# A bias column in a channel product, and PSUM copies of the first head pairs on one engine

## The chip, the cores and the metric

The kernel runs on one core of a Trainium2 chip. The metric is the device time of one execution in microseconds (us), as the median of several runs. A profile is one execution recorded by the hardware; its own time is given beside its span (first to last instruction). Engines are named as in the profile: PE is TensorE (matrix products; PEld are its weight loads), ACT is ScalarE, DVE is VectorE, POOL is GpSimd, SP is SyncE, which here only issues transfers.

## The reference, cut to what matters

Block-sparse attention, followed by a residual MLP with affine maps in place of normalisations. Batch 4, 8 heads, 768 positions, head size 64; model width 512, hidden width 2048.

```python
scores = q @ k.T / 8                      # masked by blocks of 32
attn   = softmax(where(mask, scores, -1e9))
x      = concat_heads(attn @ v)           # [4, 768, 512]
a1  = alpha1 * x + beta1
u   = x + lam * einsum('ts,bsd->btd', w_tok, a1)
a2  = alpha2 * u + beta2
out = u + lam * (relu(a2 @ w_ch1) @ w_ch2)
```

Since a2 @ w_ch1 = (alpha2 * u) @ w_ch1 + beta2 @ w_ch1, beta2 can enter as a bias of the hidden layer: a vector of 2048 numbers, beta2 @ w_ch1.

## The kernel before, in words

All work is cut into jobs, and the program order of every engine is found while the kernel is built: a list scheduler (the loop at L1100) keeps a planned time per engine (`free_at`, L253), planned durations per job, counts of free buffers (`slots`, L254), and at each planned instant gives an engine the ready job of the best priority. A job may name two engines; then whichever is free first in the plan takes it. `pin_order` (L50) fixes the order found. The plan exists only at build time; on the chip every engine runs its own queue in that order and waits for its inputs. Where the plan leaves TensorE idle before the second channel product has begun, `fill` (L173) emits matmuls on a zero tile (L171, tile `warm` to `cp`).

The attention runs over 16 pairs of heads (p = 0 to 15, four per batch element), each pair in nine units of 128x1024 scores. Pairs 0 to 5 ("single", L661): TensorE makes the transposes of a head's queries and keys in one "mm" PSUM buffer (L219), two copies bring them into `qx` and `kx` (L589, L592; the instruction is in the helper `copy`, L279 on ScalarE and L281 on VectorE), score matmuls go into one of two "sps" buffers (L676), ScalarE makes the exponentials (L691), TensorE the product with the values (L716), VectorE the normalisation (L648, L651). The mask is part of the product. Pairs 6 to 15 ("paired", L738) get their transposes from transfers issued by SyncE (L615), and VectorE applies a mask with a minimum (L785). That mask, `maskT`, is spread over the partitions by 18 transfers that SyncE issues in a row (`min_`, L506 to L517); the plan gives them 7200 ns of SyncE's time at L521.

Between attention jobs lie those of the MLP. Per pair: VectorE forms a1 (L869, L877), TensorE mixes tokens (L889, two blocks of 18 matmuls), VectorE adds to `x_sb` and scales by alpha2 (L899, L905), and the result is transposed into the tile `uT`, for the first batch element by TensorE and a copy (L926, L929), for the others by a transfer (L936). Per batch element and half of the positions (index `kk`, eight in all; `hf` says which half), 16 hidden tiles `f` follow: four matmuls of 384 columns (L962), then ReLU with the bias column `b1t[:, f]`, on ScalarE (L973) or VectorE (L977), into `hts`. The second product (L1011) makes three row blocks from `hts`, VectorE adds them to x (L1028), and SyncE stores them (L1035). While attention runs, hidden tiles share the two "mm" buffers with token mixing and transposes.

The bias `b1t` is made by four jobs of its own: beta2 comes in as `be2T` (L376), is cast to bf16 (`be2`, L452), and 64 matmuls with one column each (L464) and four copies (L473) give beta2 @ w_ch1. All hidden tiles wait for these (L986).

Of the kernel before, what the change touches and what calls it, by code (L numbers as in the profile page):

```python
# [13 lines left out]
BF = mybir.dt.bfloat16  # L14
# [6 lines left out]
S = 768  # L21
# [6 lines left out]
P = 128  # L28
# [39 lines left out]
def kernel(  # L68
# [62 lines left out]
    a2_bc = pp.tile([P, DM], FP, name="a2_bc", tag="a2_bc")  # L131
    be2T = pp.tile([P, 4], FP, name="be2T", tag="be2T")
    lam_bcb = pp.tile([P, DM], BF, name="lam_bcb", tag="lam_bcb")
    be2b = pp.tile([P, 4], BF, name="be2b", tag="be2b")
    b1t = pp.tile([P, 16], FP, name="b1t", tag="b1t")
    eqt = pp.tile([P, NR + 1, NBLK], FP, name="eqt", tag="eqt")
    mbm = pp.tile([P, NBLK], FP, name="mbm", tag="mbm")
# [112 lines left out]
    dma_free = [8000.0]  # L250
    SEM = 70.0
    DRAIN = 166.0
    free_at = dict(NONE=0.0, PE=T0, ACT=T0, DVE=T0, POOL=4800.0, SP=T0)  # L253
    slots = dict(  # L254
        sps=2, mm=2, cp=1, ops=1, eT=NET, head=NQB, vext=NV, ld=NLD, rel=3,
        x=NXB, uT=3, hts=2, a1p=2, ub=2, ot=2, w2b=1,
# [23 lines left out]
        else:  # L280
            nc.vector.tensor_copy(out=out, in_=in_)  # L281

    def Copy(prio, fn, deps, take=(), give=()):
        j = Job(("ACT", "DVE"), 550.0, prio, fn, deps, take, give)
        j.alt = ACT_COPY
        return j

# [134 lines left out]
    for t in range(NT):  # L422

        def tr(t=t):
            tl["wt", t] = tp = mm_tile([P, NT, P], BF)
            for s in range(NT):
                nc.tensor.transpose(tp[:, s, :], wtk_tile[0][:, t, s : S : NT], identb[:])

        def cp_(eng, t=t):
            copy(eng, wtokT[:, :, ts(t, P)], tl.pop(("wt", t))[:])  # L430

        j = Job("PE", mmt(NT, P), (5, t), tr, [wload["tok", t // 2]], take=("mm",))
        last = t == NT - 1
        wtok_jobs.append(
            Copy((4, t), cp_, [j], give=("mm", "w2b") if last else ("mm",))
        )
    for g in range(4):
        load_w2(g, w2_prio[g], wtok_jobs)
# [10 lines left out]
    def lamb():  # L449
        nc.vector.tensor_copy(out=lam_bcb[:], in_=lam_bc[:])  # L450

    def be2():  # L452
        nc.vector.tensor_copy(out=be2b[:], in_=be2T[:])

    j_lamb = Job("DVE", 420.0, (7, 0), lamb, [l_lam])
    j_be2 = Job("DVE", 165.0, (7, 1), be2, [l_be2])
    b1_jobs = []
    for g in range(4):

        def bmm(g=g):  # L460
            tl["bp", g] = bp = mm_tile([P, 4])
            for f in range(4):
                for dk in range(4):
                    nc.tensor.matmul(  # L464
                        bp[:, f : f + 1],
                        w1b[:, dk, ts(4 * g + f, P)],
                        be2b[:, dk : dk + 1],
                        start=(dk == 0),
                        stop=(dk == 3),
                    )  # L470

        def bcp(g=g):
            nc.vector.tensor_copy(out=b1t[:, ts(g, 4)], in_=tl.pop(("bp", g))[:])  # L473

        j = Job("PE", mmt(16, 64), (5, 20 + g), bmm, [j_be2] + [wload["w1", i] for i in range(4)], take=("mm",))
        b1_jobs.append(Job("DVE", 160.0, (3, 20 + g), bcp, [j], give=("mm",)))
    w2_jobs = []
    for g in range(8):

# [38 lines left out]

    mrow_job = j = Job("DVE", 400.0, (2, 3, 9), mrow)
    j = Job("SP", 400.0, (0, 0), mout, [j], lat=2500.0)  # L520
    j = Job("SP", 7200.0, (0, 1), min_, [j])  # L521
    j.bulk = 5500.0
    mask_jobs = [j]

# [19 lines left out]
    for p in range(len(pairs)):  # L544
        if p == 0:

            def fc():
                first_cast(1)

            def f_tr():  # L550
                tl["h0"] = transposes(rel0, 1)

            def f_cq(eng):
                copy(eng, qx[1][0:D, :], tl["h0"][0:D, :])

            def f_ck(eng):
                copy(eng, kx[1][0:D, :], tl.pop("h0")[D:P, :])

            head_ready[0] = Job("DVE", 1.0, (0, 0), lambda: None, take=("head", "rel"))
            j = Job("DVE", 720.0, (2, 0), fc)  # L560
            j = Job("PE", mmt(NT, P), (2, 0), f_tr, [j], take=("mm",))
            j = Copy((1, 0, 1), f_cq, [j, head_ready[0]], take=("head",))
            j = Copy((1, 0, 2), f_ck, [j], give=("mm", "rel"))

            def f_mb():
                nc.vector.tensor_copy(out=qx[1][MB, :], in_=qx[0][MB, :])

            jb = Job("DVE", 350.0, (2, 0, 1), f_mb)
            head_ready[1] = Job("NONE", 0.0, (0,), lambda: None, [j, jb], lat=0.0)
        elif p < NPE:  # L570

            def rel_of(p, i):
                def f():
                    if i == 0:
                        rels[p] = wk.tile([P, 2, NT, 2 * D], BF, name="rel", tag="rel", bufs=3)
                    return rels[p][:, :, :, i * D : (i + 1) * D]

                return f

            cq = cast_job(p, 0, "q2", rel_of(p, 0), (2, p, 0), ("rel",))  # L580
            ck = cast_job(p, 1, "k2", rel_of(p, 1), (2, p, 1), (), [cq])
            prev = head_ready[2 * p - 1]
            for a in range(2):
                h = 2 * p + a

                def tr(p=p, a=a, h=h):
                    tl["hd", h] = transposes(rels[p], a)

                def cpq(eng, h=h):  # L589
                    copy(eng, qx[h % NQB][0:D, :], tl["hd", h][0:D, :])  # L590

                def cpk(eng, h=h):  # L592
                    copy(eng, kx[h % NQB][0:D, :], tl["hd", h][D:P, :])

                jt = Job("PE", mmt(NT, P), (2, p, a), tr, [ck, prev], take=("mm", "head"),
                         give=("rel",) if a else ())
                j1 = Copy((1, p, a), cpq, [jt])
                j2 = Copy((1, p, a), cpk, [jt])
                prev = head_ready[h] = Job("NONE", 0.0, (0,), lambda: None, [j1, j2], give=("mm",), lat=0.0)
        else:  # L600

            def stage_of(p, i):
                def f():
                    if i == 0:
                        rels[p] = wk.tile([P, 2, NT, P], BF, name="rel", tag="rel", bufs=3)
                    return rels[p][:, i, :, :].rearrange("p o (h d) -> p h o d", h=2)

                return f

            cq = cast_job(p, 0, "q2", stage_of(p, 0), (3, p, 0), ("rel",))  # L610
            ck = cast_job(p, 1, "k2", stage_of(p, 1), (3, p, 1), (), [cq])

            def xt(p=p):
                for i, dst in enumerate((qx, kx)):
                    nc.sync.dma_start_transpose(  # L615
                        dst[slot_of(p)][:].rearrange("p (o c) -> p o c", o=NT),
                        rels[p][:, i, :, :].rearrange("p o c -> p (o c)"),
                    )

            prev = [head_ready[2 * NPE - 1]] if p == NPE else [head_ready[2 * p - 2]]  # L620
            jx = Job("SP", 2600.0, (1, p), xt, [ck] + prev, take=("head",), lat=2500.0,
                     give=("rel",))
            jx.slow = True
            head_ready[2 * p] = head_ready[2 * p + 1] = jx
# [228 lines left out]
    for p in range(len(pairs)):  # L853
# [60 lines left out]

        def ut_tile(b=b, n=n):
            if n == 0:
                uTs[b] = wk.tile([P, 4, S], BF, name="uT", tag="uT", bufs=3)
            return uTs[b]

        take = ("uT",) if n == 0 else ()  # L920
        if b == 0:
# [4 lines left out]
                    nc.tensor.transpose(up[:, t, :], tl["ub", p][:, t, :], identb[:])  # L926

            def ucp(eng, p=p, n=n, ut_tile=ut_tile):
                copy(eng, ut_tile()[:, n, :], tl.pop(("up", p))[:].rearrange("p o c -> p (o c)"))  # L929

            j = Job("PE", mmt(NT, P), (2, p, 9), utr, ubs, take=("mm",), give=("ub",))
            ut_jobs[p] = Copy((1, p, 9), ucp, [j], take=take, give=("mm",))
        else:

            def uxt(p=p, n=n, ut_tile=ut_tile):
                nc.sync.dma_start_transpose(  # L936
                    ut_tile()[:, n, :].rearrange("p (o c) -> p o c", o=NT),
                    tl["ub", p][:].rearrange("p o c -> p (o c)"),
                )

# [1 line left out]

    hts = {}
    cps = {}
    ch2_prev = {}
    for kk in range(2 * B):
        b, hf = divmod(kk, 2)
        relus = []  # L950
        for f in range(16):

            def c1(kk=kk, b=b, hf=hf, f=f):
                if f == 0:
                    hts[kk] = wk.tile([P, 16, HS], BF, name="hts", tag="hts", bufs=2)
                if tl.pop(("mmsel", kk, f)) == "sps":
# [3 lines left out]
                tl["hp", kk, f] = hp  # L960
                for dk in range(4):
                    nc.tensor.matmul(  # L962
                        hp[:, 0:HS],
                        w1b[:, dk, ts(f, P)],
                        uTs[b][:, dk, ts(hf, HS)],
                        start=(dk == 0),
                        stop=(dk == 3),
                    )

            def rl(eng, kk=kk, f=f):  # L970
                hp = tl.pop(("hp", kk, f))
                if eng == "ACT":
                    nc.scalar.activation(  # L973
                        hts[kk][:, f, :], hp[:, 0:HS], AF.Relu, bias=b1t[:, f : f + 1], scale=1.0
# [8 lines left out]
                        op1=ALU.max,  # L983
                    )

            deps = [ut_jobs[b * NPAIR + n] for n in range(NPAIR)] + b1_jobs  # L986
            if f:
                deps.append(first)
            take = ((("mm", "sps"), ("mmsel", kk, f)),) + (("hts",) if f == 0 else ())
            j = Job("PE", mmt(4, HS), (5, kk, f), c1, deps, take=take,  # L990
                    give=("uT",) if hf == 1 and f == 15 else ())
            j.ch = True
            if not f:
                first = j
            jr = Job(("ACT", "DVE"), 600.0, (0, kk, f), rl, [j], give=(("mmsel", kk, f),))
            relus.append(jr)
        last_m = None
        parts = [(m, 0, DM) for m in range(3)]
# [2 lines left out]
        for mi, (m, lo, w) in enumerate(parts):  # L1001
# [35 lines left out]
                    tl.pop(("ot", kk, mi))[:, 0:w],  # L1037
                )

            give = (("cpsel", kk, mi),) + (("x",) if hf == 1 and mi == len(parts) - 1 else ())  # L1040
            jo = Job("DVE", 155 + w / 0.96, (0, kk, mi), otf, [prev], take=("ot",), give=give)
            Job("SP", 400.0, (2, kk, mi), store, [jo], give=("ot",), lat=1600.0)

# [184 lines left out]
```

The softmax here doesn't subtract the row's maximum and nothing guards it: scores larger than these inputs give would overflow.

## Time and profile before

| | before |
|---|---|
| median of 8 runs | 318.49 us (317.64 to 319.22) |
| profiled execution | 317.67 us |
| its span | 315.9 us |
| PE busy | 307.3 us |
| DVE busy | 211.6 us |
| ACT busy | 199.3 us |
| ACT head and uT copies (L279) | 9 of about 0.79 us, and 1 |
| bias matmuls (L464) | 64 |

A row of a list in order of time gives start, duration, engine, line, operation, output from input with their shapes, a count, and in brackets the idle time before it and what ended it. A row of the chain of waits gives start, the time that this step holds the chain, engine, output, line and a count. Durations of single TensorE matmuls include their latency and overlap, so time on TensorE is read from one start to the next.

### The profile page before, as it was taken

The numbers are of one execution on the slowest core, as the hardware profiler recorded it, in microseconds if no ns is written. First come the engines' busy times: TensorE is split into PE (matmuls) and PEld (weight loads), VectorE is DVE, ScalarE is ACT, GpSimd is POOL, SyncE is SP. The second block draws the span as 40 slices with busy tenths as digits, with TensorE's granted clock in tenths as the row PEclk, the third lists the DMA queues.
The fourth block names the chain that finished last, engine by engine and source line by source line (L and its number), as shares of the span: only waits on it lengthen the run. The fifth ranks groups of instructions, "written<-read, shape, count | busy, mean of one in ns | idle before, by whom it ended". The sixth has DMA issues, their size and how long they took to land.

```text
span 315.9 us, 7689 instructions
## 1 busy us (share of the span) xinstructions
PE 307.3 (97%) x3232; PEld 189.8 (60%) x3268; DVE 211.6 (67%) x441; ACT 199.3 (63%) x253; POOL 51.4 (16%) x91
## 2 busy tenths in 40 slices
PE   8999999999999999999999999999999999999995
PEld 3667868885645655556545655566646665545444
DVE  4558987988778687788878886788859671010111
ACT  4999889987678664666677654766587502828100
POOL 5647161000211211211311210220000000000000
PEclk9999999999999999999999999999999999999999
DMA  6999999991344385716462595618210203010021
GB/s 148 184 242 216 213 191 210 180 180 27 53 77 82 55 110 106 129 23 116 95 113 34 91 117 109 121 19 117 61 25 3 58 35 91 2 66 2 33 100 66
DMA packets 47210, 30.81 MB, mean 98 GB/s; under 512 B 27552, under 2 KB 43080, under 8 KB 47176
## 3 DMA queue, kind: packets, MB, share of 16 engines
q0 software_dynamic: 15984, 15.47, 32.0%
q1 hardware_dynamic: 30940, 14.61, 20.7%
q8 instruction: 25, 0.41, 0.5%
q10 hardware_dynamic: 252, 0.24, 0.3%
q14 instruction: 9, 0.07, 0.1%
HBM read 32.04 MB, written 6.33 MB: 121 GB/s over the span
## 4 chain that ended last, share of the span: by engine, by line
PE 89%; ACT 6%; DVE 3%; issue 1%; ACTq 0%
PE mm L962 24%; PE cp L1011 21%; PE mm L889 10%; PE ops L812 8%; PE sps L754 7%; PE sps L676 6%; PE ops L1011 5%; ACT eT L691 4%; PE ops L716 3%; PE sps L962 2%; PE cp L171 2%; PE mm L219 1%; ACT kx L279 1%; ACT qx L279 1%; DVE ot L1028 1%
## 5 line engine op out<-in xcount | busy, mean ns | idle before, releaser
L780 ACT ACTIVATE eT<-sps 128x1024 f16<-128x1024 f32 x90 | 88.2, 1020 | 32.6 <-PE sps L754 30.3
L962 PE MATMUL mm<-uT,w1b 128*128 128x384 bf16 x468 | 88.4, 326 | 0.1
L973 ACT ACTIVATE hts<-mm,b1t 128x384 bf16<-128x384 f32 x82 | 47.7, 582 | 51.4 <-PE mm L962 49.6
L1011 PE MATMUL cp<-w2b,hts 128*128 128x512 bf16 (+1 forms) x289 | 71.1, 373 | 1.8
L962 PEld LDWEIGHTS <-w1b 128*128 128x128 bf16 x512 | 46.4, 98 | 32.1 <-issue 4.3
L785 DVE TENSOR_TENSOR eT<-eT,maskT 128x1024 f16<-128x1024 f16 x90 | 60.2, 683 | 3.5 <-ACT eT L780 3.4
L1011 PEld LDWEIGHTS <-hts 128*128 128x128 bf16 x400 | 36.7, 98 | 35.6 <-issue 2.1
L691 ACT ACTIVATE eT<-sps 128x1024 f16<-128x1024 f32 (+1 forms) x55 | 52.3, 1017 | 3.5 <-PE sps L676 3.2
L812 PEld LDWEIGHTS <-eT 128*128 128x128 f16 x720 | 29.5, 97 | 15.3 <-issue 4.8
L1028 DVE TENSOR_TENSOR ot<-x_sb,cp 128x512 f32<-128x512 f32 (+1 forms) x20 | 13.4, 671 | 37.0 <-PE cp L1011 36.8
L889 PE MATMUL mm<-a1p,wtokT 128*128 128x128 bf16 x576 | 36.1, 219 | 0.1
L812 PE MATMUL ops<-vext,eT 128*128 128x65 f16 x720 | 34.9, 193 | 0.0
L889 PEld LDWEIGHTS <-wtokT 128*128 128x128 bf16 x576 | 32.9, 98 | 2.7 <-issue 0.8
L977 DVE TENSOR_SCALAR hts<-mm,b1t 128x384 bf16<-128x384 f32 x35 | 21.5, 615 | 18.0 <-PE mm L962 17.9
L676 PE MATMUL sps<-qx,kx 88*128 88x512 bf16 (+1 forms) x144 | 31.5, 325 | 0.9 <-ACT eT L691 0.6
L315 POOL COPY held<-flag 1x1 bf16<-1x1 bf16 x24 | 8.6, 358 | 137.8 <-DVE flag L335 137.8
L754 PE MATMUL sps<-qx,kx 64*128 64x512 bf16 (+1 forms) x240 | 27.3, 326 | 0.0
L716 PEld LDWEIGHTS <-eT 128*128 128x128 f16 x432 | 19.0, 97 | 5.2 <-DVE x_sb L651 0.2
L899 DVE TENSOR_TENSOR x_sb<-x_sb,mm 128x384 f32<-128x384 f32 x32 | 17.6, 551 | 5.8 <-PE mm L889 5.4
L716 PE MATMUL ops<-vext,eT 128*128 128x65 f16 x432 | 20.8, 193 | 0.0
L651 DVE TENSOR_TENSOR x_sb<-ops,rcp 128x384 f32<-128x384 f32 x32 | 17.8, 557 | 1.1
L754 PEld LDWEIGHTS <-kx 64*128 64x128 bf16 x240 | 8.0, 94 | 16.5 <-issue 14.1
(71 smaller groups left out, 241.6 us busy)
## 6 DMA issues: line engine op xcount, KB each, us to landing
out_dram<-ot SPq DMA_DIRECT2D x23, 256.0 KB
v<-in_v_dram POOLq DMA_DIRECT2D x16, 192.0 KB, 4.9
q<-in_q_dram POOLq DMA_DIRECT2D x15, 192.0 KB, 4.3
k<-in_k_dram POOLq DMA_DIRECT2D x15, 192.0 KB, 3.8
w1b<-in_moe_w_ch_dram POOLq DMA_DIRECT2D x4, 512.0 KB, 10.0
w2b<-in_moe_w_ch_dram POOLq DMA_DIRECT2D x4, 512.0 KB, 11.9
wtk<-in_moe_w_tok_dram POOLq DMA_DIRECT2D x3, 384.0 KB, 9.8
maskT<-mask_rows SPq DMA_DIRECT2D x14, 72.0 KB
```

The costliest lines, as they stand in the source:

```text
L676: nc.tensor.matmul(sps[:, f - u * UN : f - u * UN + w], kx[h][0:KC, ts(jt, P)], qx[h][0:KC, c : c + w], start=True, stop=True,)
L691: nc.scalar.activation(eT[:, c], sps[:, c], AF.Exp, bias=EXPB, scale=SCALE)
L716: nc.tensor.matmul(ops[p, a][:, t * VW : t * VW + D + 1], eTs[p, u][:, ts(i - u * GU, P)], vx[:, a, jt, 0 : D + 1], start=(i % HT == 0), s ...
L754: nc.tensor.matmul(sps[:, a * 512 + lo : a * 512 + lo + w], kx[sl][r, ts(jt, P)], qx[sl][r, c : c + w], start=True, stop=True,)
L780: nc.scalar.activation(eT[:], sps[:], AF.Exp, bias=EXPB, scale=SCALE)
L785: nc.vector.tensor_tensor(out=e, in0=e, in1=maskT[:, u, :].unsqueeze(1).broadcast_to([P, 2, 512]), op=ALU.min,)
L812: nc.tensor.matmul(ops[p, a][:, t * VW : t * VW + D + 1], eTs[p, u][:, a * 512 + c * P : a * 512 + (c + 1) * P], vx[:, a, jt, 0 : D + 1], ...
L889: nc.tensor.matmul(tp[:, j, :], wtokT[:, s, ts(3 * g + j, P)], tl["a1p", p][:, s, :], start=(s == 0), stop=(s == NT - 1),)
L962: nc.tensor.matmul(hp[:, 0:HS], w1b[:, dk, ts(f, P)], uTs[b][:, dk, ts(hf, HS)], start=(dk == 0), stop=(dk == 3),)
L973: nc.scalar.activation(hts[kk][:, f, :], hp[:, 0:HS], AF.Relu, bias=b1t[:, f : f + 1], scale=1.0)
L977: nc.vector.tensor_scalar(out=hts[kk][:, f, :], in0=hp[:, 0:HS], scalar1=b1t[:, f : f + 1], scalar2=0.0, op0=ALU.add, op1=ALU.max,)
L1011: nc.tensor.matmul(cps[kk, mi][:, 0:w], hts[kk][:, nk, ts(m, P)], w2tile[0][:, nk, lo : lo + w], start=(nk == 0), stop=(nk == 15),)
```

## The change

The bias jobs go. beta2, cast to bf16, is written as column 768 of the first batch element's `uT` (whose rows grow by 16 columns). For kk = 0 the product takes 385 columns: the half that ends at position 767, so the two halves of each batch element change places. Before each of the 16 activations of kk = 0 the extra column is copied from PSUM into `b1t` on the engine that does the activation; all activations read `b1t` as before. The cast waits for the first `uT` copy, and hidden tiles wait for the cast, for the four loads of the first weights and, as before, for their `uT`.

`Copy` gets a switch `only`; with it the job's engines are VectorE and an engine "NEVER" that is never free. It is on for the query and key copies of pairs 0 to 3, off elsewhere. The plan's time for the mask's transfers becomes 15500 ns, and that of an activation of kk = 0 800 ns in place of 600.

```diff
-    free_at = dict(NONE=0.0, PE=T0, ACT=T0, DVE=T0, POOL=4800.0, SP=T0)
+    free_at = dict(NEVER=1e9, NONE=0.0, PE=T0, ACT=T0, DVE=T0, POOL=4800.0, SP=T0)
...
-        j = Job(("ACT", "DVE"), 550.0, prio, fn, deps, take, give)
+        j = Job(("DVE", "NEVER") if only else ("ACT", "DVE"), 550.0, prio, fn, deps, take, give)
...
-    j_be2 = Job("DVE", 165.0, (7, 1), be2, [l_be2])
-    b1_jobs = []
-    for g in range(4):
-
-        def bmm(g=g):
-            tl["bp", g] = bp = mm_tile([P, 4])
-            for f in range(4):
-                for dk in range(4):
-                    nc.tensor.matmul(
-                        bp[:, f : f + 1],
-                        w1b[:, dk, ts(4 * g + f, P)],
-                        be2b[:, dk : dk + 1],
...
-            nc.vector.tensor_copy(out=b1t[:, ts(g, 4)], in_=tl.pop(("bp", g))[:])
...
-    j = Job("SP", 7200.0, (0, 1), min_, [j])
+    j = Job("SP", 15500.0, (0, 1), min_, [j])
...
-            j = Copy((1, 0, 1), f_cq, [j, head_ready[0]], take=("head",))
-            j = Copy((1, 0, 2), f_ck, [j], give=("mm", "rel"))
+            j = Copy((1, 0, 1), f_cq, [j, head_ready[0]], take=("head",), only=3 >= 0)
+            j = Copy((1, 0, 2), f_ck, [j], give=("mm", "rel"), only=3 >= 0)
...
-                j1 = Copy((1, p, a), cpq, [jt])
-                j2 = Copy((1, p, a), cpk, [jt])
+                j1 = Copy((1, p, a), cpq, [jt], only=p <= 3)
+                j2 = Copy((1, p, a), cpk, [jt], only=p <= 3)
...
-                uTs[b] = wk.tile([P, 4, S], BF, name="uT", tag="uT", bufs=3)
+                uTs[b] = wk.tile([P, 4, S + 16], BF, name="uT", tag="uT", bufs=3)
...
+    def be2():
+        nc.vector.tensor_copy(out=uTs[0][:, :, S], in_=be2T[:])
+
+    j_be2 = Job("DVE", 165.0, (3, 0, 10), be2, [l_be2, ut_jobs[0]])
...
-        b, hf = divmod(kk, 2)
+        b, second = divmod(kk, 2)
+        hf = 1 - second
+        nc_ = HS + 1 if kk == 0 else HS
...
-                        hp[:, 0:HS],
+                        hp[:, 0:nc_],
                         w1b[:, dk, ts(f, P)],
-                        uTs[b][:, dk, ts(hf, HS)],
+                        uTs[b][:, dk, hf * HS : hf * HS + nc_],
...
+                if kk == 0:
+                    copy(eng, b1t[:, f : f + 1], hp[:, HS : HS + 1])
...
-            jr = Job(("ACT", "DVE"), 600.0, (0, kk, f), rl, [j], give=(("mmsel", kk, f),))
+            jr = Job(("ACT", "DVE"), 600.0 if kk else 800.0, (0, kk, f), rl, [j], give=(("mmsel", kk, f),))
```

More of the change, by code (lines that the diff above doesn't have):

```diff
@@ L133 @@
     lam_bcb = pp.tile([P, DM], BF, name="lam_bcb", tag="lam_bcb")
-    be2b = pp.tile([P, 4], BF, name="be2b", tag="be2b")
     b1t = pp.tile([P, 16], FP, name="b1t", tag="b1t")
@@ L281, in copy, with Copy @@
             nc.vector.tensor_copy(out=out, in_=in_)
-    def Copy(prio, fn, deps, take=(), give=()):
-        j = Job(("ACT", "DVE"), 550.0, prio, fn, deps, take, give)
+    def Copy(prio, fn, deps, take=(), give=(), only=False):
+        j = Job(("DVE", "NEVER") if only else ("ACT", "DVE"), 550.0, prio, fn, deps, take, give)
         j.alt = ACT_COPY
@@ L434 @@
         wtok_jobs.append(
-            Copy((4, t), cp_, [j], give=("mm", "w2b") if last else ("mm",))
+            Copy((4, t), cp_, [j], give=("mm", "w2b") if last else ("mm",), only=False)
         )
@@ L450, in lamb @@
         nc.vector.tensor_copy(out=lam_bcb[:], in_=lam_bc[:])
-    def be2():
-        nc.vector.tensor_copy(out=be2b[:], in_=be2T[:])
     j_lamb = Job("DVE", 420.0, (7, 0), lamb, [l_lam])
-    j_be2 = Job("DVE", 165.0, (7, 1), be2, [l_be2])
-    b1_jobs = []
-    for g in range(4):
-        def bmm(g=g):
-            tl["bp", g] = bp = mm_tile([P, 4])
-            for f in range(4):
-                for dk in range(4):
-                    nc.tensor.matmul(
-                        bp[:, f : f + 1],
-                        w1b[:, dk, ts(4 * g + f, P)],
-                        be2b[:, dk : dk + 1],
[L468 to L472, printed above, removed]
-            nc.vector.tensor_copy(out=b1t[:, ts(g, 4)], in_=tl.pop(("bp", g))[:])
-        j = Job("PE", mmt(16, 64), (5, 20 + g), bmm, [j_be2] + [wload["w1", i] for i in range(4)], take=("mm",))
-        b1_jobs.append(Job("DVE", 160.0, (3, 20 + g), bcp, [j], give=("mm",)))
     w2_jobs = []
@@ L928, in ucp @@
             def ucp(eng, p=p, n=n, ut_tile=ut_tile):
-                copy(eng, ut_tile()[:, n, :], tl.pop(("up", p))[:].rearrange("p o c -> p (o c)"))
+                copy(eng, ut_tile()[:, n, 0:S], tl.pop(("up", p))[:].rearrange("p o c -> p (o c)"))
             j = Job("PE", mmt(NT, P), (2, p, 9), utr, ubs, take=("mm",), give=("ub",))
@@ L936, in uxt @@
                 nc.sync.dma_start_transpose(
-                    ut_tile()[:, n, :].rearrange("p (o c) -> p o c", o=NT),
+                    ut_tile()[:, n, 0:S].rearrange("p (o c) -> p o c", o=NT),
                     tl["ub", p][:].rearrange("p o c -> p (o c)"),
@@ L941 @@
             ut_jobs[p] = Job("SP", 1300.0, (0, p), uxt, ubs, take=take, give=("ub",), lat=2500.0)
+    def be2():
+        nc.vector.tensor_copy(out=uTs[0][:, :, S], in_=be2T[:])
+    j_be2 = Job("DVE", 165.0, (3, 0, 10), be2, [l_be2, ut_jobs[0]])
+    w1_jobs = [wload["w1", i] for i in range(4)]
     hts = {}
@@ L948, with c1 @@
     for kk in range(2 * B):
-        b, hf = divmod(kk, 2)
+        b, second = divmod(kk, 2)
+        hf = 1 - second
+        nc_ = HS + 1 if kk == 0 else HS
         relus = []
         for f in range(16):
-            def c1(kk=kk, b=b, hf=hf, f=f):
+            def c1(kk=kk, b=b, hf=hf, f=f, nc_=nc_):
                 if f == 0:
@@ L984, in rl @@
                     )
-            deps = [ut_jobs[b * NPAIR + n] for n in range(NPAIR)] + b1_jobs
+            deps = [ut_jobs[b * NPAIR + n] for n in range(NPAIR)] + w1_jobs + [j_be2]
             if f:
@@ L990 @@
             j = Job("PE", mmt(4, HS), (5, kk, f), c1, deps, take=take,
-                    give=("uT",) if hf == 1 and f == 15 else ())
+                    give=("uT",) if second and f == 15 else ())
             j.ch = True
@@ L1038, in store @@
                 )
-            give = (("cpsel", kk, mi),) + (("x",) if hf == 1 and mi == len(parts) - 1 else ())
+            give = (("cpsel", kk, mi),) + (("x",) if second and mi == len(parts) - 1 else ())
             jo = Job("DVE", 155 + w / 0.96, (0, kk, mi), otf, [prev], take=("ot",), give=give)
```

## The prediction

> **What bounds the kernel now.** I read the page first: engine shares, then the slices and the clock.
>
> ```profile
> PE 307.3 (97%) x3232; PEld 189.8 (60%) x3268; DVE 211.6 (67%) x441; ACT 199.3 (63%) x253; POOL 51.4 (16%) x91
> ...
> PEclk9999999999999999999999999999999999999999
> ```
>
> TensorE looks full at full clock. Part of that is not work: the planner fills TensorE's planned idle time with matmuls on zeros (L171). So I cut the span by stage and asked for every engine in the two stretches between the first score matmul (7.39 us) and the first channel matmul (66.63 us), split where the token mixing begins (30.64), and then for L171 alone in the same two.
>
> ```profile
> 7.39:30.64 23.25, 22.49 (x290) 16.04 (x293) 15.71 (x37) 21.86 (x25) 14.10 (x23) 1.00 1.17 213
> 30.64:66.63 35.99, 35.18 (x590) 28.55 (x590) 31.27 (x71) 32.48 (x37) 8.51 (x12) 1.00 1.14 195
> ...
> 7.39:30.64 23.25, 5.46 (x18) 1.89 (x21) 1.00 1.17 213
> 30.64:66.63 35.99, 2.21 (x8) 0.81 (x9) 1.00 1.14 195
> ```
>
> Columns: stretch, length, then TensorE, weight loads, VectorE, ScalarE and GpSimd (upper pair), TensorE and weight loads (lower pair), clock, DMA share. In the first stretch ScalarE is busy 21.86 of 23.25 us, and 18 of TensorE's matmuls are padding. Their modelled 5.46 us overlap; by width at the 0.42 ns a column that the L171 forms show (507 columns 376 ns, 198 columns 247 ns) they are 3.2 us. Useful TensorE work there is 17.7 us, from the steps of the chain of waits: 21 score units of 0.445, 144 value matmuls of 0.030, twelve six-transpose groups of 0.335. So the first stretch is ScalarE's. In the second, useful work is 33 of 36 us (30 units, 240 value matmuls, eight token blocks of 1.0, nine transpose groups, the bias at 1.5): that stretch is TensorE's. Behind 66.6 us TensorE is bound to the end (39.57 of each 40 us busy, no padding).
>
> What ScalarE does in the first stretch, in order of time:
>
> ```profile
> 14.63 0.80 ACT L279 COPY kx<-mm 64x768 bf16<-64x768 bf16 x1
> 15.45 1.02 ACT L691 ACTIVATE eT<-sps 128x1024 f16<-128x1024 f32 x1
> 16.59 0.80 ACT L279 COPY kx<-mm 64x768 bf16<-64x768 bf16 x1
> 17.41 1.02 ACT L691 ACTIVATE eT<-sps 128x1024 f16<-128x1024 f32 x1
> 18.45 0.80 ACT L279 COPY kx<-mm 64x768 bf16<-64x768 bf16 x1
> ...
> 20.19 0.78 ACT L279 COPY qx<-mm 64x768 bf16<-64x768 bf16 x1
> ...
> 30.87 0.79 ACT L279 COPY qx<-mm 64x768 bf16<-64x768 bf16 x1
> ...
> 32.84 0.79 ACT L279 COPY qx<-mm 64x768 bf16<-64x768 bf16 x1 [0.26 <-PE mm L219]
> ```
>
> Head copies stand between exponentials: six of the nine ScalarE head copies belong to pairs 1 to 3, the ones that move (pair 0's already lie on VectorE). The chain of waits runs through them (16.59 to 21.6 us: copy, exponential, copy, exponential, copy). The bias product is on the chain too, in the second stretch:
>
> ```profile
> 45.48 0.38 PE mm L464 x16
> ...
> 46.55 0.38 PE mm L464 x16
> ...
> 54.45 0.38 PE mm L464 x16
> ...
> 56.67 0.38 PE mm L464 x16
> ```
>
> **The change, part by part.**
>
> *Head copies to VectorE.* Each takes ScalarE from its start to the next exponential: 0.82, 0.82, 0.82, 0.68 (four before 30.64), 0.68 and 0.69 (two behind). The four are 3.1 us, plus 0.1 waited ahead of one: 3.2 us off the bounding engine, and padding of 3.2 us on TensorE can shrink by as much. VectorE pays four more copies at about 0.53 spacing (its own took 0.55 to 0.56), 2.1 us, and has 7.5 us idle there; it also stops waiting for the partner copy:
>
> ```profile
> 21.01 0.56 DVE L281 COPY kx<-mm 64x768 bf16<-64x768 bf16 x1 [0.86 <-ACT qx L279]
> ```
>
> The two copies of a head are serialised whichever engine does them, so both on VectorE make a head ready in 1.12 us (8.79 to 9.91) against 1.39 split (16.00 to 17.39). Not all 3.2 us count: token mixing can't begin at will. Its vectors b1 and alpha1 land at 25.3 and 24.7, and four VectorE passes follow (0.68, 0.67, 0.95, 0.95), so 28.6 at the earliest, against 30.64; from 27.4 to 28.6 TensorE would have only what ScalarE feeds it, about half its time. I take 2.8. The two later copies free 1.4 us of ScalarE where TensorE is full: alone 0, with up to 0.8 of remaining padding (L171 at 35.5, 42.1, 43.1, 63.7, 64.7) within reach. I take 0.2. Sum: 3.0. Cover for VectorE in 25 to 45 us is thin (17.5 of 20 us busy before, one more us now); if it is gone, the casts and the normalisations behind the copies in its queue are late, and with them token mixing.
>
> *Bias.* Removed: 64 matmuls, 4 x 0.38 = 1.5 us of TensorE in a stretch that it bounds, and four VectorE copies of 0.15. The Trainium skill, TensorE: Matmul & The Clock Gate, section "Wait — 56ns, not 53.3ns?", has two floors for a small matmul: 25 ns, or 62 ns where the sequencer decodes. By the second, 64 would be worth 4.0 us (an estimate); the rows say 0.38/16 = 24 ns, so 1.5 stands. Added: one column in 64 matmuls, 64 x 0.42 ns = 0.03 us; odd widths (401, 355, 311) lie on the same line as even ones in L171's forms. Then one column copied per hidden tile, 16 times, ahead of the first half's activations. No such row exists on ScalarE; bounds: 0.15 (VectorE's 128x4 copy, and the constant part of ScalarE's 475 and 795 ns for 384 and 768 elements) and 0.35 (the 128x4 cast of beta2). The activation reads the column just written, so I add the 0.03 that a dependent pair shows (reciprocal 0.20, its reader 0.23 later). I take 0.25, between: 16 x 0.25 = 4 us over two engines between 66.6 and 90 us. There ScalarE is busy 16.0 of 23.6 us and VectorE 18.3, and TensorE has attention, token and value work between channel tiles; I let 0.3 us through. Bounds 0 and 16 x 0.38 = 6.1. Behind a late activation waits the next tile for one of two "mm" PSUM buffers, and with it token blocks and transposes that use the same two.
>
> *Order and waits.* The beta2 cast moves behind the first uT copy (ended 39.1); the first channel tile waits for it, but also for pair 3's uT copy at 64.92, so 25 us of cover. Swapped halves: same matmuls, same stores, x slots returned at the same count. Wider uT rows: same transfers. Cost 0 each.
>
> *SyncE's planned time for the mask, 7.2 to 15.5 us.* No instruction changes; the order does. The trace has 15.64 us (47.96 to 63.60), so the plan comes to agree with the chip. Queued behind it are the transposes of pairs 6 and 7 (63.72, 66.75), wanted by score matmuls at 76.54; the first mask use is 79.1. Ten microseconds of cover: cost 0, bounds 0.5 either way, the longest TensorE gap of these stretches gained or lost once by another interleaving.
>
> *Clock.* Less padding meets a rule that speaks against the change: the same page, "Why this matters for your kernels", wants no TensorE gap over some 3 us, or the clock halves. The longest gap in these stretches is 0.56 us and the granted clock is 1.00. By the rule one lost window of 3.4 us would cost 1.7 (estimate); by the rows nothing. The planner also pads what gaps it foresees. I take 0.
>
> Sum: -3.0 - 1.5 + 0.3 = -4.2 us. The profiled execution took 317.67 us (span 315.9, 1.8 around it), so 313.5 for it; it lay 0.8 under the median of 318.49, hence **314.3** as a median.
>
> **Rivals.**
> *Loads set the pace (0.20).* For: DMA share 1.17 and 1.14; pair 3's key load lands at 27.2 and its cast runs at 28.69, so the VectorE queue has 1.5 us before it blocks on data. Against: pair 3's heads are wanted only near 41. Then the first stretch gives 0.7: 0.7 + 1.5 = 2.2, 316.3.
> *The stage packs tighter (0.10).* ScalarE's floor from 8.0 is 51 exponentials x 0.955 (eight took 7.67) + four copies x 0.75 = 51.7 us, where it took 59.4 (to 67.4); with 1 us of waits 6.7 is had: 311.8. Against: TensorE needs 49 us of the 59 itself, with pieces that wait.
> *Nothing moves (0.04).* The new order pads what is freed: 318.4.
> *Slower (0.06).* The first half's activations hold the two "mm" buffers at 66 to 90 us. From 4.5/16 = 0.28 us per tile on TensorE's path the gain is gone; at 0.38 the cost is 6.1 and the time 318.49 - 4.5 + 6.1 = 320.1. Against: other TensorE work lies between tiles, and the planner prices the activation 0.2 higher.
>
> **How the numbers follow.** Forecast 0.60, rivals 0.20, 0.10, 0.04, 0.06. The forecast's own range is 313.0 to 315.8 (conversion of 3.2 + 1.4 us between 2 and 4, leak 0 to 0.8). Leaving out about a tenth at each end: 311.8, the tight case, to 317.2, past the load case. Measurement can't tell 0.2% (0.64 us) from nothing. Faster: 0.60 + 0.20 + 0.10 = 0.90; same 0.04; slower 0.06.
>
> **What would show it.** Right: no ScalarE L279 rows but those of pairs 4 and 5 and uT; L464 gone; the first channel matmul near 62.4 instead of 66.6; fewer L171 rows before 30 us; the remainder from there to the end as long as before, within 0.5 us. Wrong if the first channel matmul is early but the end is not (work pushed behind), if VectorE shows waits on DMA at 25 to 30 us, or if TensorE shows idle time at channel tiles of the first half.

## The result and the profile after

The changed kernel takes 315.85 us in the median, the kernel before 318.46 us in the runs beside it: ratio 0.9911, 95% interval 0.9894 to 0.9928, that is 2.8 us less. (The ratio leaves out one run of the changed kernel in a slower state, 319.56 us, so it is not quite the quotient of the two medians.) The forecast was 4.2 us less, 314.3; 315.85 lies in the range of 311.8 to 317.2. The profiled execution took 316.02 us, its span is 314.3 us.

The two stretches of the prediction, all engines of the changed kernel, columns as before:

```profile
7.39:30.64 23.25, 23.14 (x321) 16.85 (x323) 18.60 (x40) 22.59 (x26) 14.85 (x23) 1.00 1.17 212
30.64:66.63 35.99, 35.47 (x546) 28.66 (x547) 31.02 (x69) 33.03 (x40) 8.69 (x12) 1.00 1.18 196
```

and its padding (now L170) alone in the same two:

```profile
7.39:30.64 23.25, 4.37 (x14) 1.47 (x16) 1.00 1.17 212
30.64:66.63 35.99, 1.07 (x5) 0.61 (x7) 1.00 1.18 196
```

Padding fell from 5.46 + 2.21 to 4.37 + 1.07 us, and 26 ScalarE instructions fit in the first stretch where 25 did. The gain shows less in their number than in what they are. ScalarE of the changed kernel in order of time:

```profile
8.02 17.03 ACT L666 ACTIVATE eT<-sps 128x512 f16<-128x512 f32 x19 [0.68 <-PE sps L651]
24.93 0.82 ACT L278 COPY wtokT<-mm 128x768 bf16<-128x768 bf16 x1
25.61 7.61 ACT L666 ACTIVATE eT<-sps 128x1024 f16<-128x1024 f32 x8
33.06 0.85 ACT L278 COPY wtokT<-mm 128x768 bf16<-128x768 bf16 x1
33.74 4.09 ACT L666 ACTIVATE eT<-sps 128x1024 f16<-128x1024 f32 x4
```

No head copy stands between exponentials up to 39 us. By 33.2 us the exponentials of 26 units are done (the 19 of the first row are 18 units, since the first unit comes in two halves; eight follow); before, the 26th ended at 40.0 us. So attention is 6.8 us ahead. Token mixing, which the prediction wanted to begin at 28.6, begins at 34.19 (before: 30.64), right behind the last copy of the mixing weights `wtokT`, which the new order puts on ScalarE behind those eight exponentials (33.06): the planner spent the freed time on attention first. The first channel product starts 6.4 us earlier, before and after:

```profile
66.46 0.81 PE L962 MATMUL mm<-uT,w1b 128*128 128x384 bf16 x4
...
60.10 0.82 PE L946 MATMUL mm<-uT,w1b 128*128 128x385 bf16 x4
```

Little of that lead is left a moment later. The first paired scores start at 74.31 (before: 76.54), and the span ends 1.6 us earlier. What happens between is in TensorE's and VectorE's orders of time; first TensorE of the changed kernel:

```profile
69.87 0.81 PE L946 MATMUL mm<-uT,w1b 128*128 128x385 bf16 x4 [1.51 <-DVE x_sb L874]
...
72.05 1.47 PE L946 MATMUL mm<-uT,w1b 128*128 128x385 bf16 x8 [0.93 <-DVE x_sb L874]
```

then VectorE:

```profile
68.99 0.36 DVE L504 COPY rel<-q 128x768 bf16<-128x768 bf16 x1 [3.10 <-DMA q<-in_q_dram]
69.27 0.55 DVE L874 TENSOR_TENSOR x_sb<-x_sb,mm 128x384 f32<-128x384 f32 x1
...
71.17 0.36 DVE L809 COPY vext<-v 128x768 f16<-128x768 f16 x1 [0.52 <-DMA v<-in_v_dram]
71.45 0.55 DVE L874 TENSOR_TENSOR x_sb<-x_sb,mm 128x384 f32<-128x384 f32 x1
```

VectorE stands 3.1 us at the cast of pair 7's queries, whose load has not landed. Behind that cast in its queue is the addition (L874) that empties a token block's "mm" buffer; the next channel tile needs the buffer, and TensorE idles 1.51 us, then 0.93 us behind the value load in the same way. The kernel before casts pair 7's queries at 66.26 us, 1.5 us after the load had landed (64.7). Its cast, its issue of the load, and the issue in the changed kernel:

```profile
66.26 0.35 DVE L529 COPY rel<-q 128x768 bf16<-128x768 bf16 x1
...
46.16 0.76 POOL L317 DMA_DIRECT2D q<-in_q_dram  x1
...
51.35 0.70 POOL L316 DMA_DIRECT2D q<-in_q_dram  x1 [5.92 <-DVE rel L504]
```

The load is issued 5.2 us later because the load buffer that it takes over is freed by pair 5's query cast (`rel`, L504), at 50.71 us here and 45.28 before.

### The profile page after: what moved, and what is told of

Same layout as the page of the kernel before. It is cut to its first block, busy times and chain, and to the rows that moved or that the text cites. A ratio compares the mean times of both kernels' runs of the same rounds, so it can differ in the third digit from the quotient of the medians.

```text
span 314.3 us, 7542 instructions
## 1 busy us (share of the span) xinstructions
PE 303.7 (97%) x3160; PEld 187.2 (60%) x3197; DVE 213.7 (68%) x447; ACT 198.1 (63%) x259; POOL 52.4 (17%) x91
## 4 chain that ended last, share of the span: by engine, by line
PE 80%; DMA 12%; issue 3%; DVE 2%; ACT 1%; POOL 1%; POOLq 0%
PE mm L946 23%; PE cp L997 21%; DMA v<-in_v_dram 10%; PE ops L787 8%; PE sps L729 7%; PE mm L864 7%; PE ops L997 5%; PE sps L946 2%; PE sps L651 2%; DMA q<-in_q_dram 2%; PE cp L170 2%; PE ops L691 1%; PE mm L218 1%; DVE ot L1014 1%; POOL k L316 0%
## 5 line engine op out<-in xcount | busy, mean ns | idle before, releaser
L946 PE MATMUL mm<-uT,w1b 128*128 128x384 bf16 (+1 forms) x468 | 88.8, 326 | 3.0 <-DVE x_sb L874 2.4
L314 POOL COPY held<-flag 1x1 bf16<-1x1 bf16 x24 | 9.3, 389 | 131.1 <-DVE flag L334 131.1
L874 DVE TENSOR_TENSOR x_sb<-x_sb,mm 128x384 f32<-128x384 f32 x32 | 17.6, 550 | 4.6 <-PE mm L864 4.2
```

The lines of the kernel that those rows point to most:

```text
L946: nc.tensor.matmul(hp[:, 0:nc_], w1b[:, dk, ts(f, P)], uTs[b][:, dk, hf * HS : hf * HS + nc_], start=(dk == 0), stop=(dk == 3),)
```

## The experiments

The theory: ScalarE relieved is the gain, the late load takes part of it back. Against it stood: the bias product is the gain; the column copies cost; the loads bound everything. Ratios are to the kernel before, with 95% intervals; 0.001 is 0.32 us.

**The copies alone.** The kernel before with `only` for pairs 0 to 3 and nothing else.

```diff
...
-                j1 = Copy((1, p, a), cpq, [jt])
-                j2 = Copy((1, p, a), cpk, [jt])
+                j1 = Copy((1, p, a), cpq, [jt], only=p <= 3)
+                j2 = Copy((1, p, a), cpk, [jt], only=p <= 3)
```

> The kernel before, with only the switch for the query and key copies of pairs 0 to 3 (VectorE only); the bias product and the halves stay as they were. Theory (head copies stand between exponentials, their removal is worth 3.0 us before the token mixing begins, and late loads of pair 7 give part back): ratio 0.990 to 0.994, first channel product well ahead of 66.5 us. Rival (the bias product alone is the gain, the copies only move padding): 1.000 +- 0.002. Rival (the parts add up to the whole measured 2.8 us): this one 1.3 us, ratio 0.996.

Measured: 0.9967 (0.9950 to 0.9985), 1.0 us. Smaller than expected, and the runs spread from 314.6 to 320.9 us. The profiled execution is the fastest of them: its query load, issued at 51.35 as well, landed at 65.3, and TensorE was idle for only 0.24 us. It does not show the typical run.

**The bias column alone.** The changed kernel with `only` off.

```diff
...
-                j1 = Copy((1, p, a), cpq, [jt], only=p <= 3)
-                j2 = Copy((1, p, a), cpk, [jt], only=p <= 3)
+                j1 = Copy((1, p, a), cpq, [jt], only=False)
+                j2 = Copy((1, p, a), cpk, [jt])
```

> The changed kernel with the query and key copies of pairs 1 to 3 given to either engine again, so that the bias column is the only part of the change. Theory: TensorE loses 64 one-column matmuls worth 1.5 us and pays 0.3 us for the column copies, ratio 0.996. Rival (the column copies hold the two PSUM buffers of the first half): 1.000 or above, with idle TensorE at the channel tiles of the first half.

Measured: 1.0164 (1.0135 to 1.0193), 5.2 us slower. The rival's "1.000 or above" takes the number in, but neither theory had its size or its cause. The same wait again, with the casts of pair 7 now ahead of a channel activation (VectorE waits 3.6 and 1.5 us). TensorE idles 4.05 us for that activation, and then something further happens. TensorE in order of time:

```profile
73.56 1.47 PE L946 MATMUL mm<-uT,w1b 128*128 128x385 bf16 x4 [4.05 <-DVE hts L963]
```

and all engines in stretches behind the gap (the first figure after the five engines is the granted clock):

```profile
74.00:76.00 2.00, 2.00 (x15) 1.48 (x14) 1.93 (x5) 0.00 (x0) 0.00 (x0) 0.50 1.00 223
...
78.00:80.00 2.00, 2.00 (x25) 1.70 (x24) 0.90 (x3) 1.78 (x2) 0.00 (x0) 0.69 0.00 0
80.00:82.00 2.00, 2.00 (x41) 1.59 (x39) 1.49 (x3) 1.02 (x1) 0.00 (x0) 1.00 0.00 0
```

After 4 us of idling TensorE works at half its clock for some 6 us (73.6 to 79.2): about 3 us more on top of the gap, an estimate that takes all of this work to be at half speed. This is the slowest of the six runs (325.3 us, mean clock 0.989). Four others had a mean clock of 0.995 and took 322.7 to 324.4 us, and the one at 1.000 took 321.9: most of the 5.2 us is not the clock.

**Additions ahead of casts.** The plan is told that pair 7's loads land 4 us later. On TensorE, ScalarE and GpSimd the order stays as in the changed kernel; on VectorE the token additions move ahead of pair 7's casts, and on SyncE one transpose of `uT` ahead of pair 7's.

```diff
-            ld[p, nm].late = 1500.0 if hold_ else 0.0
+            ld[p, nm].late = 1500.0 if hold_ else 4000.0 if p == 7 else 0.0
```

> The changed kernel; the plan alone is told that pair 7's three loads land 4 us later, which puts VectorE's two token additions (and the products behind them) ahead of pair 7's casts. TensorE, ScalarE and GpSimd keep their order. Theory (the casts wait for a late load at 66 to 69 us and hold VectorE's queue, so that the token blocks' PSUM buffers stay taken and TensorE stands idle 1.5 and 0.9 us): the idle time at the channel tiles goes, ratio to the changed kernel about 0.993 (2.4 us less), so 0.983 to 0.985 against the kernel before. Rival (the loads themselves are the bound, whatever stands behind the casts): the idle time moves to the paired scores of pair 7, no gain over the changed kernel (0.991).

Measured: 0.9867 (0.9850 to 0.9885), 4.2 us under the kernel before and 1.4 us under the changed one, where 2.4 was expected. VectorE of this kernel:

```profile
66.44 0.55 DVE L874 TENSOR_TENSOR x_sb<-x_sb,mm 128x384 f32<-128x384 f32 x1
...
67.97 0.55 DVE L874 TENSOR_TENSOR x_sb<-x_sb,mm 128x384 f32<-128x384 f32 x1
68.44 0.35 DVE L504 COPY rel<-q 128x768 bf16<-128x768 bf16 x1
```

The load is issued as late as in the changed kernel (51.39). It landed at 67.6 in this run; VectorE, free at 65.9 as there, would in the old order have stood some 1.7 us (an estimate from these times). Now nobody waits for it, and the first paired scores start at 71.59. The four runs lie between 313.3 and 314.3 us, where the twenty of the changed kernel spread from 313.9 to 319.6; the four further kernels below that have both the copies and the additions first ran four times each, and each kept within 0.8 us. The wait is thus the cause of the missing 1.4 us, and of the spread: how long it lasts hangs on when a transfer lands.

**No column copies**, first in the order of the changed kernel, with the bias a tile of zeros (beta2's share is missing).

```diff
-                if kk == 0:
-                    copy(eng, b1t[:, f : f + 1], hp[:, HS : HS + 1])
...
+    nc.vector.memset(b1t[:], 0.0)
```

> The changed kernel without the 16 copies of the bias column; the bias is a tile of zeros set once, so beta2's share of the hidden layer is left out. Order as planned with the copies. Theory (16 copies lie beside other work; 0.3 us leaks): ratio to the changed kernel 0.998 to 1.0. Rival (each holds a PSUM buffer of the first half on TensorE's path, 0.2 us apiece): 0.99, that is 3 us less.

Measured: 0.9887 (0.9858 to 0.9917). The interval holds both "no cost" and 1.7 us; with the load wait in the kernel this can't be told. The last experiment repeats it without that wait.

**The bias column alone, additions first.** The third edit on top of the second.

> The bias column alone (as in the run of 1.0164), with the plan told that pair 7's loads land 4 us later, so that the channel activation and the token products come ahead of pair 7's casts on VectorE. The order of the other engines changes with it, in the stretch behind. Theory (what made the bias alone slow is the wait of VectorE's queue for pair 7's loads, 3.6 and 1.5 us, with a channel activation behind it and TensorE idle for 4.1 us): about 4 to 5 us less, ratio 1.000 to 1.004. Rival (it is the added padding alone, 60 filler matmuls in place of 46, about 3 us): stays at 1.012 or above.

Measured: 1.0054 (1.0036 to 1.0072), 3.5 us less than without the additions first. That the wait made it slow is confirmed, but less falls than was expected, and the number lies between the theory's and the rival's. The profiled run has waits of its own: VectorE waits 5.0 us for the loads of the second channel weights, TensorE is busy 3.21 us of those from 60 to 65, and in the 5 us after its clock is 0.67. Its longest wait near there, and all engines in those 5 us:

```profile
PE ops L691 <- DVE x_sb L626: 1.7, 1, 1.7
...
65.00:70.00 5.00, 5.00 (x48) 3.60 (x47) 2.82 (x6) 3.29 (x6) 0.00 (x0) 0.67 1.20 129
```

Behind this gap of 1.7 us (61.7 to 63.5) the clock stood at 0.50 from 64.9 to 68.3. The run is the slowest of the six (321.42 us, mean clock 0.995); the others had 0.998 to 1.000, so the clock is no part of the median. How much of the remaining 1.7 us is the wait for the weights, and how much the padding, was not tried.

**The bias left out.** The kernel before in its own order, without the 64 matmuls and four copies (beta2's share is missing).

```diff
-                    nc.tensor.matmul(
-                        bp[:, f : f + 1],
-                        w1b[:, dk, ts(4 * g + f, P)],
-                        be2b[:, dk : dk + 1],
...
-            nc.vector.tensor_copy(out=b1t[:, ts(g, 4)], in_=tl.pop(("bp", g))[:])
+            tl.pop(("bp", g))
```

> The kernel before in its own order, with the 64 one-column matmuls and their four copies left out and the bias a tile of zeros, so beta2's share is missing. Theory (1.5 us of TensorE in a stretch that TensorE bounds): 0.995 to 0.996. Rival (ScalarE bounds that stretch, or the late loads catch up the gain): 0.998 to 1.000.

Measured: 1.0008 (0.9990 to 1.0025): nothing. All engines in the 15 us that hold these matmuls, of the kernel before:

```profile
45.00:60.00 15.00, 15.00 (x279) 12.46 (x277) 12.34 (x31) 13.77 (x16) 3.31 (x5) 1.00 1.22 203
```

and of the one without them:

```profile
45.00:60.00 15.00, 14.20 (x214) 11.22 (x214) 12.57 (x29) 14.10 (x16) 3.91 (x6) 1.00 1.20 200
```

TensorE drops to 14.20, ScalarE rises from 13.77 to 14.10. These 15 us do not hold quite the same work in both, so I compare from the exponential run at 43.56 to that at 59.96 before, 16.40 us, and from 44.21 to 60.28 here, 16.07: of 1.5 us, 0.3 shortens the stretch. ScalarE in it, first before, then here:

```profile
43.56 6.78 ACT L691 ACTIVATE eT<-sps 128x1024 f16<-128x1024 f32 x7
...
44.21 6.55 ACT L683 ACTIVATE eT<-sps 128x1024 f16<-128x1024 f32 x7
...
54.08 5.61 ACT L683 ACTIVATE eT<-sps 128x1024 f16<-128x1024 f32 x6
```

Here the exponentials of a row start 0.92 us apart (before 0.96), and 0.90 is the closest that they come anywhere in the two traces. So ScalarE's exponentials pace these rows, and 0.04 us apiece was all that could be won. Between rows ScalarE waits for TensorE, 1.1 us in all with the bias product and without: a token block stands ahead of the scores there. TensorE's own waits for exponentials over the same work, before and here (us in total, times, the longest):

```profile
PE sps L676 <- ACT eT L691: 0.6, 1, 0.6
...
PE sps L668 <- ACT eT L683: 0.8, 2, 0.6
```

They grow by 0.2 us. The remaining 1.0 us is in no row: it lies in gaps too short for the views and under durations that overlap. One doubt stays with this run: VectorE also waits 1.5 us for pair 7's value load (before 0.3) and TensorE 0.3 us behind it, so late loads may have taken the 0.3 us back. The pair of runs with the additions first, below, has no such wait. The full TensorE row of before, 15.00 of 15.00, had not said so: durations of matmuls overlap, and a modelled end fills small gaps.

**A seventh load buffer**, in the changed kernel's order, so that pair 7's query load needs not wait for pair 5's cast.

```diff
-                nm, pair_ap(src, *pairs[p]), [P, 2, NT * D], dt, "ld", NLD,
+                nm, pair_ap(src, *pairs[p]), [P, 2, NT * D], dt, "ld", 7,
...
-    nc.gpsimd.tensor_copy(out=hold[:], in_=rel0[:, 0, 0, 0:NBLK])
+    nc.gpsimd.tensor_copy(out=lam_bcb[:, 0:NBLK], in_=rel0[:, 0, 0, 0:NBLK])
```

> The changed kernel in its own order on every engine, with a seventh buffer for loads that the plan does not know of; a small helper tile is put into an existing one for its room. Pair 7's query load no longer waits for pair 5's query cast. Theory (the load is late because it is issued late, at 51.35 in place of 46.2): issued near 45.5, lands by 66, TensorE's idle 1.5 us at the channel tile goes but the key and value loads still wait for casts at 50.7 and 51.8, so the 0.9 stays: ratio 0.986 to 0.988 against the kernel before. Rival (the transfers in flight are the bound, not the issue): the load lands as late as it did, 0.991.

Measured: 0.9900 (0.9872 to 0.9928). The load is issued at 45.33 in place of 51.35, 6 us earlier, and its cast still waits, 1.73 in place of 3.10 us, until 67.69: 1.3 us are won on 6. TensorE's first gap (1.51 us) is gone; the second, behind the casts of key and value, grows from 0.93 to 1.54. In the median that can't be told from the changed kernel (0.9911). The load now takes 22.3 us from issue to landing, where it took 17.6 in the changed kernel. So of the lateness most is transfers in flight, not the issue: the rival's side. Which transfers hold it was not tried.

**Seventh buffer and additions first.**

> Both: the seventh load buffer and the token additions ahead of pair 7's casts. Theory: with the additions first nothing that TensorE needs soon stands behind the casts, so the earlier load adds nothing: 0.985 to 0.988, as with the additions alone. Rival (pair 7's transposes are still late for its scores): a further 0.002 to 0.004.

Measured: 0.9835 (0.9816 to 0.9854), runs of 312.9 to 313.4 us: 5.3 us under the kernel before, the lowest ratio of all kernels run, with nothing left out of what it computes. Against the additions alone (0.9867) the intervals overlap by a hair; a further 1 us is likely and not shown. It beats both kernels.

**The copies, additions first**, with the bias product as it was:

> The kernel before with the VectorE-only copies and the token additions ahead of pair 7's casts; bias product as before. To compare with the changed kernel with the additions first (0.9867). Theory (with ScalarE relieved TensorE bounds the second stretch, so the 64 bias matmuls are worth something only in company with the copies): 0.990 to 0.992, that is 1.0 to 1.5 us more than 0.9867. Rival (the bias column is worth nothing in any company, as it was worth nothing in the order of before): 0.986 to 0.988.

Measured: 0.9865 (0.9838 to 0.9892), against 0.9867 with bias column and all. TensorE, ScalarE and GpSimd have the order of the copies alone (0.9967); about a quarter of the 4.3 us reached that kernel, the rest was lost to the order around the casts.

**The same, without bias matmuls and column copies** (beta2's share is missing):

> As the one before it, in the same order, with the 64 one-column matmuls and their four copies left out and the bias zero (beta2's share missing), and no column copies either. Theory (removal on TensorE's path): 1.0 to 1.5 us less than with them. Rival (ScalarE's exponentials still pace the stretch): within 0.3 us of it.

Measured: 0.9861 (0.9834 to 0.9887), 0.1 us less, and the runs of both kernels mix. The removal is worth nothing that shows in this company either; TensorE's waits for exponentials up to 72 us become 1.6 us, from 0.4, and VectorE waits no longer than 0.2 us for a load of pair 7 in either profile.

**The copies on VectorE in the plan of before.**

```diff
                 def cpq(eng, h=h):
...
+                    eng = "DVE" if p <= 3 else eng
```

> The kernel before in its own order; only the six copies of pairs 1 to 3 that the plan gives to ScalarE are issued on VectorE, at the place that the plan has for them. Padding, and what stands behind what on TensorE, stay. Theory (the gain needs a new order: the padding and TensorE's order were laid for the slower ScalarE): half the gain of the copies or less, 0.997 to 1.000. Rival (ScalarE's time itself is the gain): 0.990.

Measured: 1.0007 (0.9993 to 1.0021): nothing. ScalarE is relieved of the six copies and waits instead. Its waits up to 66 us, in the kernel before:

```profile
ACT eT L691 <- PE sps L676: 3.2, 6, 0.9
```

and here:

```profile
ACT eT L693 <- PE sps L678: 8.0, 12, 1.2
```

ScalarE here in order of time, with three of those waits:

```profile
18.75 1.02 ACT L693 ACTIVATE eT<-sps 128x1024 f16<-128x1024 f32 x1 [0.83 <-PE sps L678]
20.64 1.02 ACT L693 ACTIVATE eT<-sps 128x1024 f16<-128x1024 f32 x1 [0.87 <-PE sps L678]
22.86 8.62 ACT L693 ACTIVATE eT<-sps 128x1024 f16<-128x1024 f32 x9 [1.19 <-PE sps L678]
```

4.8 us of waiting stand where 4.5 us of copies stood: TensorE's queue, padding and all, keeps the pace of the old plan. The gain needs the new order.

**Additions first, no column copies** (beta2's share is missing):

> The changed kernel with the additions first and without the 16 copies of the bias column (bias zero, beta2's share missing). Theory (the column copies lie beside other work): 0.9857 to 0.987, within 0.3 us of 0.9867. Rival (each holds a PSUM buffer of the first half): 0.98.

Measured: 0.9842 (0.9816 to 0.9868), against 0.9867 with the columns: 0.8 us, and the intervals overlap: between nothing and some 2 us; that much stays open.

## Why the prediction was right, and where it was not

The median fell in the range, close to the load case (316.3). Two of the three signs that were to show it wrong came all the same: the first channel product is early (6.4 us) and the end is not (1.6 us), and TensorE stands idle at channel tiles of the first half. By the prediction's own steps:

- **Head copies, 3.0 us.** Too small, and for another reason: 4.3 us with the additions first (0.9865). What the additions first alone do to the kernel before was not tried; in its profile VectorE waits only 0.3 us for pair 7's loads, so little is there to be won. The step had ScalarE's freed time shrink the padding before 30.64, and token mixing begin at 28.6. In fact token mixing began later, at 34.2, and attention ran ahead by 6.8 us. And freed time as such is worth nothing (1.0007): the order that the planner then writes is the gain.
- **Bias, 1.5 us.** Wrong: nothing that shows, in two kept orders (1.0008; 0.9861 against 0.9865). The step that failed was the view ahead of it, "that stretch is TensorE's". I counted 33 us of useful work in 36 and took the full row for the bound; the exponentials paced most of it. ScalarE's 32.48 of 36 stood in the same line. What a plan laid without the product gains is less sure: with the copies and the additions first, it is 0.9842 without column copies against 0.9865 with the product, 0.7 us with overlapping intervals. With the column copies, as forecast at 1.2 us together, nothing is left (0.9867).
- **Column copies, 0.3 us.** The rows are 0.16 us (ScalarE) and 0.15 (VectorE) where I took 0.25; the whole is between 0 and 2 us, with 0.8 in the middle.
- **The load.** The missing term, 1.4 us (0.9911 against 0.9867). The rival "Loads set the pace" had the mechanism, VectorE's queue blocked by a cast, at pair 3 and 27 us; it came with pair 7 at 66 us. I had checked where loads were just in time in the trace of before, and not which load is issued later when a cast that frees its buffer moves back.
- **The mask's planned time.** I let it change the order. It changes none: the program that the planner writes has the same order on every engine with 7200 or 15500 ns, with the copies or without, with the bias column or without.
- **Clock.** 0 was right for the profiled execution (0.999) and not for all. Four runs of the changed kernel had a mean clock of 0.987 to 0.994 and took 317.3 to 319.6 us; the sixteen at 0.998 or above took 313.9 to 317.0. Of the copies alone, seven of 22 runs had 0.989 to 0.995. None of the twenty runs with copies and additions first fell below 0.998. So the late load seems to cost some runs the clock as well; none of these has a trace, and it is not shown. The rule that I set aside (the Trainium skill, TensorE: Matmul & The Clock Gate, section "Why this matters for your kernels": no idle gaps over some 3 us) agrees with the 0.50 behind the gap of 4.05 us in the bias column alone. It does not foresee the 0.50 behind a gap of 1.7 us in the bias column alone with the additions first, while gaps of 1.51 and 0.93 us in the changed kernel left the clock at 1.00. I should have looked at the waits that the change could bring, not at those of before.

So -4.2 as a sum was what the changed kernel has without the wait (0.9867), put together from a term too small, one of which nothing shows and one not resolved. That they add up is luck; the wait then took 1.4 of it.

## What to carry to other kernels

Where a program's order is laid by a plan, time freed on one engine is worth only what the new order makes of it: compare against the same edit in the old order before crediting the edit. A queue runs in order, so a wait for a transfer costs what stands behind it; put what others need ahead of a cast whose load may be late, and ask of every moved cast which load takes over its buffer. A full TensorE row in a profile does not prove that TensorE is the bound: leave some of its work out in the same order, and see whether the stretch that holds the same work gets shorter.

## What the hardware showed that I had not expected

After TensorE had idled 4.05 us (in the kernel with the bias column alone) its granted clock was 0.50 for some 6 us, while it was busy without a gap; by the estimate of 3 us one wait cost nearly twice its length. Behind a gap of 1.7 us it was 0.50 for 3.4 us as well (bias column alone, additions first, the slowest of its runs), and behind one of 1.54 us (seventh buffer) it stayed at 1.00. And issuing a load 6 us earlier, with a DMA share of 1.21 between 45 and 60 us (1.28 in the changed kernel), let its cast begin only 1.3 us earlier.
